# Loads on one queue in order of use, attention spread over the steps, and the LayerNorm statistics one step later

## Chip, cores, metric

One core of one Trainium2 chip. The metric is the device time of one execution in microseconds (us), lower is better. A single run over 1.5% above the fastest run of its kernel is called slow, and slow runs are left out of the ratios.

## The reference

Attention without softmax, an RMS norm of each head, then a two-layer MLP whose activation is h times softmax(h), with a LayerNorm in front of the second layer.

```python
kv  = einsum('bhsd,bhse->bhde', k, v)            # 8 batches, 8 heads, 576 tokens, 64 wide
out = einsum('bhsd,bhde->bhse', q, kv)
x   = out / sqrt(mean(out*out, -1) + 1e-6) * g_norm   # then [4608, 512]
h   = x @ w_in                                   # [4608, 1024]
solu = h * softmax(h)
ln  = (solu - mean(solu)) / sqrt(var(solu) + 1e-6) * g_ln
return ln @ w_out                                # [4608, 512]
```

## The kernel before

It works through nine blocks of 512 tokens: 512 of each of the eight batches, and a ninth block of what is left over. A block has eight pieces, each one `h_step` (four matmuls, exponential on ACT, product on DVE, square on POOL). I call eight pieces a stage. Stage c computes h of block c, the output of block c-1, and the attention of block c+1. LayerNorm is folded away: the second layer runs on u = h*exp(h) with centred weights, and each row is scaled at the end by a factor that needs three sums over its 1024 columns.

```python
def h_step(c, f):
    ...
    nc.scalar.activation(out=e[:, f % 2, :], in_=t[:, :], func=AF.Exp, ...)
    nc.vector.tensor_tensor(out=u_sb[c][:, f, :], in0=t[:, :], in1=e[:, f % 2, :], op=MUL)
    nc.gpsimd.tensor_tensor(out=usq_sb[c][:, f, :], in0=u_sb[c][:, f, :], in1=u_sb[c][:, f, :], op=MUL)
    if f % 2 == 1:
        nc.gpsimd.tensor_tensor(out=es_sb[c][:, f // 2, :], in0=e[:, 0, :], in1=e[:, 1, :], op=ADD)

def stats(c):
    ...   # 20 matmuls add usq, u and es into sum_ps
    nc.vector.tensor_copy(sums[:, :], t[:, :])
    st_ps = pst.tile([128, 4, 3], FP32, name="st_ps", tag="st")
    for m in range(4):
        nc.tensor.matmul(st_ps[:, m, :], sums[:, m * 128:(m + 1) * 128], stat_pick[:, :], ...)
    ...   # st, sq, var, vare on DVE; lv (Ln), rstd (Exp) on ACT

for c in range(NC + 1):
    for s in range(8):
        if c < NC: h_step(c, s)
        if c >= 1 and s == 0: stats(c - 1)       # sums, copy and transposition in one go
        if c == 0: ...   # s 0..3: scale w_out on POOL; s 5: its mean on PE; s 6, 7: centre it on DVE
        ...              # attention of block c+1: qT at 0 and 1, s_mm and o_mm at 2..5, kv at 6
        ...              # loads of block c+3 at s 2, 3, 4, issued by POOL
        if c >= 1:
            out_half(c - 1, s // 2, s % 2)
            if s % 2 == 1: out_evac(c - 1, s // 2)
```

The softmax here doesn't subtract the row's maximum and nothing guards it: scores larger than these inputs give would overflow.

## Time and profile before

| | before |
|---|---|
| time, median of 4 runs beside the changed kernel | 288.5 us (287.4 to 290.0) |
| span of the profiled run | 290.9 us (its time was 292.74, a slow run) |
| busy: PE, POOL, DVE, ACT | 220.5, 171.8, 140.0, 123.1 us |
| first h of stage 0 (its end), of stage 1 (its start) | 39.7, 66.8 us |

Here are the page's head, its first DMA queue, and one group of its costliest instructions: line, engine, operation, tiles, count, then busy time and mean in ns, then idle time before them.

```profile
span 290.9 us, 3927 instructions
...
PE 220.5 (76%) x1528; PEld 102.2 (35%) x1528; DVE 140.0 (48%) x251; ACT 123.1 (42%) x199; POOL 171.8 (59%) x171
...
q0 software_dynamic: 37632, 14.16, 42.1%
...
L269 ACT ACTIVATE lv<-vare,zero_t 128x4 f32<-128x4 f32 x9 | 2.7, 297 | 51.0 <-DVE vare L265 51.0
```

PE is busy for 76% of the span, but work that runs at half clock counts as busy too. The queue `q0`, which POOL issues, carries 14.2 MB; all weights come by another. The last line is the first half of the chain to the row factor: ACT waits 51.0 us for it in nine stages, so each of them stands at the end of a long chain.

The profiled run is a slow one, 4 us longer than the median. Stage lengths of before that are quoted below are of this slow run, and can be too long by 4 us in all.

### The profile page before, as it was taken

The numbers are of one execution on the slowest core, as the hardware profiler recorded it, in microseconds if no ns is written. First come the engines' busy times: TensorE is split into PE (matmuls) and PEld (weight loads), VectorE is DVE, ScalarE is ACT, GpSimd is POOL, SyncE is SP. The second block draws the span as 40 slices with busy tenths as digits, with TensorE's granted clock in tenths as the row PEclk, the third lists the DMA queues.
The fourth block names the chain that finished last, engine by engine and source line by source line (L and its number), as shares of the span: only waits on it lengthen the run. The fifth ranks groups of instructions, "written<-read, shape, count | busy, mean of one in ns | idle before, by whom it ended". The sixth has DMA issues, their size and how long they took to land.

```text
span 290.9 us, 3927 instructions
## 1 busy us (share of the span) xinstructions
PE 220.5 (76%) x1528; PEld 102.2 (35%) x1528; DVE 140.0 (48%) x251; ACT 123.1 (42%) x199; POOL 171.8 (59%) x171
## 2 busy tenths in 40 slices
PE   0014487455899799979897989899799798989792
PEld 0013033122444254434344434444344353344240
DVE  0503444309357325754672366357456646626422
ACT  1000738421087117713940394077169239513100
POOL 8624139997179907962994386257545727719700
PEclk9999999959599859997996699799999979979979
DMA  6999990296019901990796079101210201101114
GB/s 124 298 318 194 197 170 0 22 150 66 0 38 188 192 3 38 186 157 2 114 197 104 1 113 209 41 36 37 74 37 36 74 0 72 66 9 72 72 39 109
DMA packets 45763, 28.05 MB, mean 96 GB/s; under 512 B 15024, under 2 KB 39600, under 8 KB 45744
## 3 DMA queue, kind: packets, MB, share of 16 engines
q0 software_dynamic: 37632, 14.16, 42.1%
q1 hardware_dynamic: 8112, 13.64, 14.1%
q8 instruction: 12, 0.20, 0.3%
q14 instruction: 7, 0.06, 0.1%
HBM read 32.51 MB, written 9.44 MB: 144 GB/s over the span
## 4 chain that ended last, share of the span: by engine, by line
PE 37%; POOL 24%; ACT 13%; DMA 10%; DVE 7%; issue 6%; POOLq 0%; ACTq 0%; DVEq 0%
PE out_ps L280 14%; PE h_ps L227 10%; POOL usq_sb L236 9%; DMA vs<-in_v_dram 6%; POOL es_sb L238 6%; ACT e_sb L234 5%; PE st_ps L257 4%; DMA ks<-in_k_dram 4%; POOL w_out_g L320 4%; ACT rst L214 3%; PE qT_ps L184 3%; DVE u_sb L235 3%; ACT lss L212 3%; ACT osq L206 3%; DVE sums L254 2%
## 5 line engine op out<-in xcount | busy, mean ns | idle before, releaser
L236 POOL TENSOR_TENSOR usq_sb<-u_sb 128x512 bf16<-128x512 bf16 x72 | 75.0, 1043 | 87.4 <-DVE u_sb L235 87.3
L227 PE MATMUL h_ps<-x_sb,w_in_sb 128*128 128x512 bf16 x288 | 80.7, 405 | 0.8 <-DVE x_sb L215 0.8
L280 PE MATMUL out_ps<-w_out_sb,u_sb 128*128 128x512 bf16 x288 | 80.7, 411 | 0.0
L235 DVE TENSOR_TENSOR u_sb<-h_ps,e_sb 128x512 bf16<-128x512 f32 x72 | 49.6, 688 | 55.4 <-ACT e_sb L234 55.3
L234 ACT ACTIVATE e_sb<-h_ps,zero_t 128x512 f32<-128x512 f32 x72 | 49.3, 685 | 61.9 <-PE h_ps L227 61.9
L238 POOL TENSOR_TENSOR es_sb<-e_sb 128x512 bf16<-128x512 f32 x36 | 45.9, 1275 | 0.0
L227 PEld LDWEIGHTS <-w_in_sb 128*128 128x128 bf16 x288 | 29.8, 104 | 40.8 <-issue 12.0
L280 PEld LDWEIGHTS <-u_sb 128*128 128x128 bf16 x288 | 28.5, 104 | 37.2 <-issue 11.7
L215 DVE TENSOR_TENSOR x_sb<-o_ps,rst 128x512 bf16<-128x512 f32 x36 | 24.9, 691 | 34.2 <-ACT rst L214 34.2
L206 ACT ACTIVATE osq<-o_ps,zero_t 128x512 bf16<-128x512 f32 x36 | 24.2, 674 | 29.7 <-PE o_ps L199 29.7
L288 DVE TENSOR_SCALAR ob<-out_ps,rstd 128x512 f32<-128x512 f32 x36 | 26.7, 743 | 6.4 <-PE out_ps L280 6.4
L212 ACT ACTIVATE lss<-s_ps,eps_t 128x512 f32<-128x512 f32 x36 | 24.6, 683 | 10.4 <-PE s_ps L210 10.4
L214 ACT ACTIVATE rst<-lss,zero_t 128x512 f32<-128x512 f32 x36 | 26.0, 722 | 1.2
L269 ACT ACTIVATE lv<-vare,zero_t 128x4 f32<-128x4 f32 x9 | 2.7, 297 | 51.0 <-DVE vare L265 51.0
L210 PE MATMUL s_ps<-osq,head_mean 128*128 128x512 bf16 x36 | 14.7, 407 | 12.4 <-ACT osq L206 9.6
L152 PE MATMUL kv_ps<-vs,ks 128*64 128x64 bf16 x256 | 6.7, 214 | 15.7 <-DMA vs<-in_v_dram 15.7
L257 PE MATMUL st_ps<-stat_pick,sums 128*128 128x3 f32 x72 | 12.2, 292 | 7.2 <-DVE sums L254 7.2
L257 PEld LDWEIGHTS st_ps<-stat_pick,sums 128*128 128x128 f32 x72 | 11.4, 241 | 17.0 <-DVE sums L254 17.0
L249 PE MATMUL sum_ps<-usq_sb,stat_sel 128*32 128x512 bf16 x72 | 10.4, 384 | 8.8 <-POOL usq_sb L236 8.8
L184 PE MATMUL qT_ps<-ident,qs 128*64 128x128 bf16 x256 | 14.7, 285 | 2.6 <-DMA qs<-in_q_dram 2.6
L199 PE MATMUL o_ps<-qT_sb,kvbd 128*128 128x512 bf16 x32 | 13.5, 428 | 1.6 <-ACT lss L212 1.6
L189 DVE COPY qT_sb<-qT_ps 128x1024 bf16<-128x1024 bf16 x18 | 12.3, 685 | 4.4 <-PE qT_ps L184 4.1
(50 smaller groups left out, 149.7 us busy)
## 6 DMA issues: line engine op xcount, KB each, us to landing
out_dram<-ob SPq DMA_DIRECT2D x32, 256.0 KB, 2.3
ks<-in_k_dram POOLq DMA_DIRECT2D x8, 512.0 KB, 6.2
vs<-in_v_dram POOLq DMA_DIRECT2D x8, 512.0 KB, 9.7
qs<-in_q_dram POOLq DMA_DIRECT2D x8, 512.0 KB, 9.1
w_in_f<-in_moe_w_in_dram SPq DMA_DIRECT2D x4, 512.0 KB, 7.6
w_out_f<-in_moe_w_out_dram SPq DMA_DIRECT2D x4, 512.0 KB, 11.4
out_dram<-ob SPq DMA_DIRECT2D x8, 128.0 KB, 2.3
krem<-in_k_dram POOLq DMA_DIRECT2D x8, 64.0 KB, 12.4
```

Source lines behind the costliest of these rows:

```text
L206: nc.scalar.activation(out=osq[:, :], in_=t[:, :], func=AF.Square, bias=zero_t[:, :])
L212: nc.scalar.activation(out=lss[:, :], in_=t[:, :], func=AF.Ln, bias=eps_t[:, :])
L214: nc.scalar.activation(out=rst[:, :], in_=lss[:, :], func=AF.Exp, scale=-0.5, bias=zero_t[:, :])
L215: nc.vector.tensor_tensor(out=x_sb[c][:, p, :], in0=o_ps.pop(p)[:, :], in1=rst[:, :], op=MUL)
L227: nc.tensor.matmul(t[:, :], w_in_sb[:, dt, f * 128:(f + 1) * 128], x_sb[c][:, dt, :], start=(dt == 0), stop=(dt == NP - 1),)
L234: nc.scalar.activation(out=e[:, f % 2, :], in_=t[:, :], func=AF.Exp, bias=zero_t[:, :])
L235: nc.vector.tensor_tensor(out=u_sb[c][:, f, :], in0=t[:, :], in1=e[:, f % 2, :], op=MUL)
L236: nc.gpsimd.tensor_tensor(out=usq_sb[c][:, f, :], in0=u_sb[c][:, f, :], in1=u_sb[c][:, f, :], op=MUL)
L238: nc.gpsimd.tensor_tensor(out=es_sb[c][:, f // 2, :], in0=e[:, 0, :], in1=e[:, 1, :], op=ADD)
L257: nc.tensor.matmul(st_ps[:, m, :], sums[:, m * 128:(m + 1) * 128], stat_pick[:, :], start=True, stop=True)
L280: nc.tensor.matmul(t[:, :], u_sb[c][:, f, m * 128:(m + 1) * 128], w_out_sb[:, f, :], start=(f == 0), stop=(f == NF - 1),)
L288: nc.vector.tensor_scalar_mul(out=ob[:, :], in0=t[:, :], scalar1=rstd_sb[c][:, m:m + 1])
```

## The change

The intent: no load ahead of its use (one queue, in order of first use, w_in cast in flight and not scaled separately), no wait for the statistics (sums one piece later, their transposition two), and attention in even portions. The scheduling becomes a table of (stage, piece). Cut to its core:

```diff
-    for dt in range(NP):
-        nc.sync.dma_start(w_in_f[:, dt, :], moe_w_in[dt * 128:(dt + 1) * 128, :])
+    load_kv(0)
+    load_q(0)
+    for half in range(2):
+        nc.gpsimd.dma_start(w_in_sb[:, :, cols], moe_w_in[:, cols].rearrange("(n p) f -> p n f", p=128))
 ...
+    load_kv(1)
+    load_q(1)
+    for f4 in range(2):
+        nc.gpsimd.dma_start(w_out_f[:, 4 * f4:4 * f4 + 4, :], ...)
+    load_kv(2)
+    load_q(2)
 ...
-        t = pat.tile([128, NP, 128], FP32, name="kv_ps", tag="at")     # qT_ps likewise
+        t = pst.tile([128, NP, 128], FP32, name="kv_ps", tag="st")
 ...
-        nc.vector.tensor_tensor(out=x_sb[c][:, p, :], in0=o_ps.pop(p)[:, :], in1=rst[:, :], op=MUL)
+        nc.vector.scalar_tensor_tensor(
+            out=x_sb[c][:, p, :], in0=o_ps.pop((c, p))[:, :], scalar=g_rep[:, :], in1=rst[:, :], op0=MUL, op1=MUL
+        )
 ...
+    at(0, 3, kv_mm, 1) ...            # attention of block 1: kv 3, qT 4 and 5, s and o in 5 to 7
+    for f in range(NF):
+        at(0, 4 + f // 4, w_out_scale, f, nc.vector if f % 2 else nc.gpsimd)
+    at(0, 6, w_out_mean)
+    for f in range(NF):
+        at(0, 7, w_out_center, f)
+    for a in range(2, NC):
+        at(a - 2, 4 if a > 2 else 7, kv_mm, a)      # and kv_evac
+        at(a - 2, 5 if a > 2 else 7, qT, a, 0)
+        at(a - 2, 6 if a > 2 else 7, qT, a, 1)
+        at(a - 2, 7, o_mm, a, 0)
+        for p in range(NP):
+            at(a - 1, 2 * p, s_mm, a, p)
+            if p + 1 < NP:
+                at(a - 1, 2 * p + 1, o_mm, a, p + 1)
+    for c in range(NC):
+        at(c, 0, load_kv, c + 3); at(c, 1, load_q, c + 3); at(c, 2, load_rem, qrem, ...)
+        ...
+        at(c + 1, 1, stats, c)          # now only sums and their copy
+        at(c + 1, 2, stats_t, c)        # transposition and the row factor
+        at(c + 1, 3, out_evac, c, 0)    # then 4, 6, 7
```

## The prediction

> **What bounds the kernel now.** I read the page's rows of slices first (who is busy, at what clock), then the waits of all engines (who holds TensorE up), then the timeline of one block of 512 tokens and of the start, and last short stretches with their granted clock. I call a block's eight pieces of work (one `h_step` each) a stage; stage 0 fills the pipe, stages 1 to 8 are steady, stage 9 drains.
>
> ```profile
> PE   0014487455899799979897989899799798989792
> POOL 8624139997179907962994386257545727719700
> PEclk9999999959599859997996699799999979979979
> ```
>
> A slice is 7.3 us. PE is busy from the fifteenth slice on, but every third or fourth slice its granted clock is 5 to 7 tenths. The waits say what stands in front of those slices:
>
> ```profile
> PE kv_ps L152 <- DMA vs<-in_v_dram: 15.7, 1, 15.7
> PEld st_ps L257 <- DVE sums L254: 17.0, 9, 2.2
> PE s_ps L210 <- ACT osq L206: 9.6, 23, 1.3
> PE sum_ps L249 <- POOL usq_sb L236: 8.8, 12, 2.5
> PE mean_ps L326 <- POOL w_out_g L320: 7.1, 3, 5.2
> ```
>
> Once a stage, right after its first piece, PE wants the statistics of the block before. It waits for the last squares from POOL, then 0.8 us for the copy of the sums on DVE, with nothing else to do. The timeline around 100 us and the stretches show what this costs beyond the wait itself:
>
> ```profile
> 99.63 0.43 PE L249 MATMUL sum_ps<-usq_sb,stat_sel 128*32 128x512 bf16 x1 [0.61 <-POOL usq_sb L236]
> 102.23 1.87 PE L257 MATMUL st_ps<-stat_pick,sums 128*128 128x3 f32 x8 [0.78 <-DVE sums L254]
> ...
> 98.00:100.00 2.00, 0.74 (x9) 0.35 (x12) 0.50 (x1) 0.00 (x0) 2.00 (x3) 0.96 1.61 229
> 100.00:102.00 2.00, 1.45 (x13) 0.20 (x5) 0.51 (x1) 0.00 (x0) 1.81 (x2) 0.50 0.67 148
> 106.00:108.00 2.00, 2.00 (x7) 0.61 (x5) 0.00 (x0) 0.00 (x0) 0.00 (x0) 0.50 0.00 0
> ```
>
> PE was busy 0.74 of two us, then the clock is 0.50 until about 110, so roughly 10 us of work runs at half speed: four h matmuls take 1.71 us in the chain there, 0.86 to 0.88 elsewhere. The starts of the copy of `sums` give the stage lengths: 73.47, 101.49, 128.78, 156.04, 183.35, 208.66, 231.38, 255.35, 275.19, that is 28.0, 27.3, 27.3, 27.3, 25.3, 22.7, 24.0 and 19.8 us. The steady part is bound by PE, its waits, and the slow clock after them; the long stages are those whose loads keep POOL late. In pieces 2 to 5 ACT is nearly full (1.97 of 2.00 us from 86 to 92), and they last 2.5 to 2.9 us.
>
> The start is bound by loads. `vs` of block 0 reaches PE at 15.68 and its remainder at 22.90, as four loads of w_in and four of w_out share the engines. A second wait there matters for the change:
>
> ```profile
> 9.94 0.91 POOL L74 DMA_DIRECT2D ks<-in_k_dram  x1
> 12.90 0.87 POOL L74 DMA_DIRECT2D vs<-in_v_dram  x1 [2.06 <-DMA ks<-in_k_dram]
> 15.92 0.88 POOL L74 DMA_DIRECT2D qs<-in_q_dram  x1 [2.15 <-DMA vs<-in_v_dram]
> 31.54 0.88 POOL L74 DMA_DIRECT2D qs<-in_q_dram  x1 [1.91 <-DMA vs<-in_v_dram]
> ```
>
> The 9th load of POOL's queue starts when the 1st has landed, the 10th when the 2nd has, the 17th when the 9th has. POOL never has more than eight in flight, and it stands still meanwhile, its arithmetic too.
>
> **What the Trainium skill says.** "TensorE: Matmul & The Clock Gate", Part 1: PE's clock is gated to half unless the array was busy in the last window of about 3.4 us. The trace agrees: 0.50 follows the poor stretch, and 1.00 returns after some 10 us here. "DMA: Bandwidth & Descriptors", "Issuing engines are not separate DMA queues": queues interleave on the same 16 engines. The trace agrees: `ks` of block 0 took 11.4 us from issue, and the median of eight such loads is 6.2. "Perfetto Trace Analysis", "Identifying the Most-Contended Engine": matmul busy time overstates, as matmuls overlap. So I count starts: four h matmuls are 1.03 us busy, but the next group starts 0.86 after them.
>
> **The change, part by part.**
>
> Steady stages. Nothing is removed from PE; the order changes. By starts at full clock: h and out 16 groups of 0.863 = 13.8; eight s and o matmuls of 0.216 = 1.7; sums 20 at 0.055 and a gap of 0.1 = 1.2; `st_ps` 1.0; transposes 2 x 0.57 = 1.1; kv 0.9. Sum 19.8 us. Statistics now come after the second piece, some 3 us later than before, while POOL needs about 2.3 us (1.04 + 1.25) after the last u: that wait goes, and with it the slow clock. The copy of sums hides under piece 2 (1.9 us of PE work against 0.7). Attention has s in even and o in odd pieces, so ACT has 3.5 us per two pieces where PE has 3.9 or more. I followed one stage in order by these durations and found two new waits. First, the four small DVE operations on `st` stand behind x of piece 2, which waits for Ln and Exp; the two small ACT operations follow, and Exp of piece 3 and the square after it stand behind those, so s in piece 4 waits about 1.1 us. Second, `kv_evac` stands behind x of piece 4, and the transposes now use the same single PSUM buffer: about 0.7 us. So 19.8 + 1.8 = 21.6, say 21.7. POOL has 8.3 + 5.0 + at most 5.6 of issuing = 18.9 us, below that. Stage 6 has no kv (20.3), stage 7 no transposes (19.0), stage 8 no attention (16.5); stage 1 starts at half clock, +1.5. Sum: 23.2 + 4 x 21.7 + 20.3 + 19.0 + 16.5 = 165.8 us. Before, the first h of stage 1 starts at about 66.8 and the last h ends at 270.9: 204.1.
>
> g_norm on x: x becomes the form that `w_out_sb` shows at 0.74 instead of 0.69 us; 36 x 0.05 = 1.8 us of DVE, off the path. Four w_in scalings of 0.77 go.
>
> The end. Before, 20.0 us from the last h to the end. Now two halves of an output tile (1.7 us) run before the sums and one between sums and `st_ps`; the third tile then waits about 1.4 us for the first one's buffer. By the same following, 17.4.
>
> The start. One queue, one load (0.5 MB written from 1 MB read) per 2.7 us, as v1 follows k1 follows q0 before (25.9, 28.8, 31.5); the 64 KB pieces 0.5. From 1.24 plus 6 us: k0 7, v0 10, remainders 11, q0 13.5, w_in 19, k1 21.6, v1 24.3, q1 28, w_out 30.7 and 33.4, k2 36, v2 39, q2 42.6. Block 0's chain from first o to last x lasts 11 us (27.8 to 39.1 before), so first h ends near 28 and not 39.7. **But this is given back.** POOL does the square of piece 0 and then issues k3, v3 and two remainders, whose eighth predecessors are q1, w_out, w_out and k2: it is held to 36. After that it still has in its queue, ahead of w_out's last scaled piece, five squares, three pair sums, three more issues, and four scalings of 1.56: 5.2 + 3.8 + 2.4 + 6.2 = 17.6, so about 54. The mean of w_out (piece 6) is PE's next work and ends near 55. Piece 7 then holds in line: h at half clock 1.7; three rounds of s, Ln, Exp, square, o at 2.8 = 8.4 to x at about 65.5; eight centrings on DVE of 0.69 = 5.5, to 71; kv copy 0.9; two transposes at half clock, each followed by its copy through the one buffer, 3.4. First h of stage 1: 75.3, against 66.8. The start loses 8 us where it means to win 11.
>
> Sum: 75.3 + 165.8 + 17.4 = 258.5 us of span against 290.9. The timed median before is 288.83, or 0.993 of that span: 257 us.
>
> **Rivals.**
> - **The start hurts less or more.** If POOL is not held by the eight in flight, the mean comes near 45 and stage 1 starts near 62 to 65: 245. For it: loads may land faster without mixing. Against: the four lines above. If POOL's scalings are slowed by DVE's own four scalings beside them, 80 and 262.
> - **DVE and ACT in line become the bound.** Each wait I found comes from a strict order behind x, and x waits 2 us for ACT. Were it 3.5 us a stage in place of 1.8, eight stages cost 14 more: 270. For it: three consumers now share the one `st` buffer and need five turns a stage. Against: DVE has about 15 us and ACT 14 of work in 21.7.
> - **The clock does not come back.** If waits of 1 us are enough to halve it once a stage, each stage keeps 4 to 5 us: about 290, same as before. Against: from 195 to 222 the clock is 1.00 with waits of 0.3 to 0.8 us.
> - **All hides.** PE at its floor of 19.8 and a start as meant: about 235 to 240. Against: the single buffer and the order on DVE.
>
> **Range and chances.** The start is uncertain by 8 us either way, the steady part by 1 us a stage, about 7; together some 10. Time 257 us, range 247 to 269. Slower or within 2% needs two rivals at once, so faster by over 2% has 0.95, within 2% 0.04, slower 0.01.
>
> **What would show it.** Right: PE's clock near 1.00 from about 80 us on; copies of `sums` 21 to 22.5 us apart; no wait of `sum_ps` on POOL above 0.5 us; s waiting on osq once a stage; `mean_ps` waiting for w_out_g by over 10 us until about 55; POOL's issues of the remainders of block 3 waiting for w_out and k2; first h near 28 and stage 1 not before 70. Wrong: stage 1 starting before 65 or after 80, stages above 23 us, or 0.5 in the clock row after 85 us.

## The result, and the profile after

| | before | after |
|---|---|---|
| median of 4 runs, all fast | 288.5 us | 261.55 us (261.12 to 263.62) |
| ratio of fast runs | | 0.908 (95%: 0.901 to 0.914) |
| profiled span | 290.9 (slow) | 258.9 (fast) |
| first h of stage 0 (its end), of stage 1 (its start) | 39.7, 66.8 | 29.9, 76.84 |
| starts of `sums`, first and last | 73.47, 275.19 | 83.08, 246.28 |

Ratios are the mean time of one kernel's fast runs over the mean of the other's of the same rounds, so they are not quite the ratio of the medians. The four matmuls of the first h start in parts, as x comes: from 36.67 to 39.13 before, from 26.84 to 29.36 after. The predicted time was 257 us, the range 247 to 269.

The page of the kernel after, the same parts as before:

```profile
span 258.9 us, 3911 instructions
...
PE 197.2 (76%) x1528; PEld 93.5 (36%) x1528; DVE 145.9 (56%) x258; ACT 122.2 (47%) x199; POOL 166.8 (64%) x170
...
PE   0244793244259899979979979998997998997972
...
POOL 8543469983005976995997797565585584695800
PEclk9999999555559999999999999999999999999997
...
q0 software_dynamic: 39232, 17.30, 51.2%
...
L275 ACT ACTIVATE lv<-vare,zero_t 128x4 f32<-128x4 f32 x9 | 2.7, 297 | 20.9 <-DVE vare L271 20.9
```

PE is counted busy for 23 us less on the same 1528 matmuls, which fits the better clock (part of it may be the slow run before). From slice 13 on (a slice is 6.5 us) the clock row holds 9 up to the last slice. The five slices with 5 are the start, where PE now waits. `q0` carries the weights too. ACT's wait for the row factor fell from 51.0 to 20.9 us.

The waits of the kernel after (engine, tile and line, releaser: us in total, times, longest):

```profile
PE mean_ps L311 <- POOL w_out_g L304: 12.4, 4, 8.6
...
PE s_ps L210 <- ACT osq L206: 11.3, 10, 1.8
...
PE qT_ps L184 <- DVE kvbd L170: 8.9, 7, 7.1
...
PEld st_ps L263 <- DVE sums L256: 0.3, 1, 0.3
```

The wait of `st_ps` for the sums is 0.3 us in all, where it was 17.0 for the weight loads alone. `sum_ps` waits for POOL no more. What is left in the steady part is s behind its square and the transposes behind the copy of kv. The largest wait is now the mean of w_out in stage 0. In the timeline (start, duration, engine, line, then in brackets the idle time before it and who ended it), POOL first, PE after it:

```profile
34.64 0.69 POOL L82 DMA_DIRECT2D krem<-in_k_dram  x1 [0.34 <-DMA w_out_f<-in_moe_w_out_dram]
37.09 0.68 POOL L82 DMA_DIRECT2D vrem<-in_v_dram  x1 [1.76 <-DMA ks<-in_k_dram]
```

```profile
49.62 1.01 PE L311 MATMUL mean_ps<-w_out_g,col_mean 128*128 128x512 bf16 x2 [8.59 <-POOL w_out_g L304]
...
73.59 1.07 PE L184 MATMUL qT_ps<-ident,qs 128*64 128x128 bf16 x16 [7.09 <-DVE kvbd L170]
...
76.84 1.91 PE L229 MATMUL h_ps<-x_sb,w_in_sb 128*128 128x512 bf16 x4
...
111.28 0.38 PE L210 MATMUL s_ps<-osq,head_mean 128*128 128x512 bf16 x1 [1.39 <-ACT osq L206]
```

POOL's remainders of block 3 waited for w_out and ks as predicted, though only 0.34 and 1.76 us. The mean waited 12.4 us for the scaled weights (8.59, 0.54, 2.76, 0.53) and ended at 57.3. Centring ran from 67.33 to 72.67, the transposes of block 2 stood behind it for 7.09 us, and stage 1 began at 76.84. In the steady part, `s_ps` at 111.28 waits 1.39 us once a stage.

The starts of `sums` are 83.08, 104.30, 126.16, 148.02, 169.88, 191.09, 211.45, 230.07 and 246.28: stages of 21.2, 21.9, 21.9, 21.9, 21.2, 20.4, 18.6 and 16.2 us. Eight stages take 163.2 us, where before had 201.7 in its slow run. The start takes 9.6 us more (83.08 against 73.47), and the end, after the last copy of the sums, 3.1 less.

### The profile page after: what moved, and what is told of

The parts are those of the page before. It is cut to its first block, busy times and chain, and to the rows that moved or that the text cites. A ratio compares the mean times of both kernels' runs of the same rounds, so it can differ in the third digit from the quotient of the medians.

```text
span 258.9 us, 3911 instructions
## 1 busy us (share of the span) xinstructions
PE 197.2 (76%) x1528; PEld 93.5 (36%) x1528; DVE 145.9 (56%) x258; ACT 122.2 (47%) x199; POOL 166.8 (64%) x170
## 4 chain that ended last, share of the span: by engine, by line
PE 48%; ACT 18%; DVE 15%; POOL 9%; issue 4%; DMA 4%; POOLq 0%; ACTq 0%; DVEq 0%
PE h_ps L229 18%; PE out_ps L286 16%; ACT rst L214 5%; ACT lss L212 5%; PE qT_ps L184 4%; DVE x_sb L215 4%; ACT e_sb L236 4%; DMA qs<-in_q_dram 4%; PE sum_ps L251 4%; POOL usq_sb L238 3%; PE s_ps L210 2%; POOL w_out_g L304 2%; DVE kvbd L170 2%; DVE w_out_sb L314 2%; POOL es_sb L240 2%
## 5 line engine op out<-in xcount | busy, mean ns | idle before, releaser
L238 POOL TENSOR_TENSOR usq_sb<-u_sb 128x512 bf16<-128x512 bf16 x72 | 75.8, 1054 | 64.3 <-DVE u_sb L237 64.2
L229 PE MATMUL h_ps<-x_sb,w_in_sb 128*128 128x512 bf16 x288 | 78.7, 399 | 0.9 <-DVE x_sb L215 0.8
L286 PE MATMUL out_ps<-w_out_sb,u_sb 128*128 128x512 bf16 x288 | 73.2, 379 | 3.7 <-DVE ob L294 3.7
L215 DVE SCALAR_TENSOR_TENSOR x_sb<-o_ps,g_rep,rst 128x512 bf16<-128x512 f32 x36 | 27.0, 750 | 29.3 <-ACT rst L214 29.3
L229 PEld LDWEIGHTS <-w_in_sb 128*128 128x128 bf16 x288 | 28.5, 104 | 39.0 <-issue 12.0
L286 PEld LDWEIGHTS <-u_sb 128*128 128x128 bf16 x288 | 26.5, 98 | 37.3 <-issue 8.6
L212 ACT ACTIVATE lss<-s_ps,eps_t 128x512 f32<-128x512 f32 x36 | 24.6, 684 | 3.1 <-PE s_ps L210 3.1
L184 PE MATMUL qT_ps<-ident,qs 128*64 128x128 bf16 x256 | 11.9, 244 | 12.6 <-DVE kvbd L170 8.9
L184 PEld LDWEIGHTS <-qs 128*64 128x64 bf16 x256 | 9.4, 124 | 18.5 <-issue 16.2
L152 PEld LDWEIGHTS <-ks 128*64 128x64 bf16 x256 | 5.5, 123 | 23.2 <-issue 9.6
L311 PE MATMUL mean_ps<-w_out_g,col_mean 128*128 128x512 bf16 x8 | 4.0, 608 | 12.4 <-POOL w_out_g L304 12.4
L275 ACT ACTIVATE lv<-vare,zero_t 128x4 f32<-128x4 f32 x9 | 2.7, 297 | 20.9 <-DVE vare L271 20.9
```

The lines of the kernel that those rows point to most:

```text
L184: nc.tensor.transpose(t[hh * 64:hh * 64 + 64, pp, cols], qs[c][:, 2 * p + hh, j, :], ident[:, :])
L212: nc.scalar.activation(out=lss[:, :], in_=t[:, :], func=AF.Ln, bias=eps_t[:, :])
L215: nc.vector.scalar_tensor_tensor(out=x_sb[c][:, p, :], in0=o_ps.pop((c, p))[:, :], scalar=g_rep[:, :], in1=rst[:, :], op0=MUL, op1=MUL)
L229: nc.tensor.matmul(t[:, :], w_in_sb[:, dt, f * 128:(f + 1) * 128], x_sb[c][:, dt, :], start=(dt == 0), stop=(dt == NP - 1),)
L286: nc.tensor.matmul(t[:, :], u_sb[c][:, f, m * 128:(m + 1) * 128], w_out_sb[:, f, :], start=(f == 0), stop=(f == NF - 1),)
```

## The experiments

Eleven kernels ran, all correct. The "delayed-statistics kernel" is the first of them. My theory: the delayed statistics give the gain, by way of the clock; the start gives part of it back through POOL's queue, the mean and the centring; the steady part is left with a wait for s and one for kv. The rivals: the even attention or the order of loads gives the gain; the wait itself and not the clock is the cost; the start is bound by loads. Ratios are against before in the same rounds, three rounds unless said. In the first batch (delayed statistics alone, without the delay, loads later, centring later) the recorded ratios work out to a mean of 290.4 us for before, above each of its fast runs there (287.46 to 288.67), so slow runs are in that mean. Against those fast runs alone the four ratios are 0.905, 0.968, 0.883 and 0.897; the order of the kernels stays.

### The delayed statistics alone

```diff
-            if c >= 1 and s == 0:
-                stats(c - 1)
 ...
-                if s % 2 == 1:
-                    out_evac(c - 1, s // 2)
+                if s == 1: stats(c - 1)
+                if s == 2: stats_t(c - 1)
+                if s in (3, 4, 6, 7): out_evac(c - 1, {3: 0, 4: 1, 6: 2, 7: 3}[s])
```

(on the kernel before, with `stats` split in two as in the change)

> The kernel before with one part of the change alone: the sums are taken after the second piece of a stage, their transposition after the third piece, the output tiles scaled one step later. Theory (the wait for POOL at the sums, and the half clock that follows it, made the long stages): the clock row stays near full from stage 2 on, stages shrink from 25 to 28 us to about 22 to 23 (pieces 2 to 5 stay limited by ACT at 2.5 us), so 8 stages save about 25 us and the end about 2: 262 us. Rival (the loads that keep POOL busy are the cause, or ACT bounds the stages anyway): stages stay above 25 us in stages 1 to 5, total above 278 us.

Measured: 261.89 us, ratio 0.898 (0.886 to 0.911), span 256.9. Its clock row:

```profile
PEclk9999999996899999999999999999999999999997
```

(The profiled run is the fastest of its kernel, 3.1 us below the other two fast ones, at a clock of 0.981 against 0.965 and 0.966.) No half clock after the start. Stages are 22.1 five times, then 20.7, 19.6 and 16.2; `sums` starts at 77.13 first and 244.02 last. This one part has the whole gain. Against the changed kernel: the start is 5.95 us earlier (77.13 and 83.08), the eight stages take 166.9 us in place of 163.2, and the end is 0.3 us longer. So, in these two traces, the rest of the change wins 3.7 us in the steady part and loses 6 in the start; which part of the rest wins it is not separated here.

### The change without the delay

```diff
+        at(c + 1, 0, stats, c)
+        at(c + 1, 0, stats_t, c)
 ...
-        at(c + 1, 1, stats, c)
-        at(c + 1, 2, stats_t, c)
-        at(c + 1, 3, out_evac, c, 0)     # and 4, 6, 7
+            at(c + 1, 2 * m + 1, out_evac, c, m)
```

> The changed kernel with that part alone undone: sums and their transposition in the first piece again, output tiles scaled at the odd pieces. Theory: the wait on POOL and the 0.8 us for the copy of the sums come back in each stage, and with them the half clock; stages 25 to 27 us where loads run, 288 us or more in all, that is, nearly all of the gain is lost. Rival (spreading the attention is what gains): stages 22 to 23.5 us, total 265 to 272.

Measured: 279.42 us, ratio 0.961 (0.950 to 0.972). The direction is right and the size a miss: 18 of 27 us are lost, not all. Its profiled run was a slow one, so only the kinds of wait are read from it:

```profile
PEld st_ps L263 <- DVE sums L256: 20.0, 9, 2.6
...
PE sum_ps L251 <- POOL usq_sb L238: 1.5, 3, 0.9
```

The wait for the copy of the sums is back (17.0 before). The wait of the sums for POOL's squares is not: 1.5 us here, 8.8 before. I had expected both. The five full stages were 23.0 to 26.4 us in that slow run. So some 9 us remain won without the delay; I had put that down as none. Part of it is probably this wait: POOL issues the loads in pieces 0 to 2 now, not 2 to 4, and has caught up by the end of the stage. That was not tested alone, and neither was the even attention, which keeps ACT from filling pieces 2 to 5.

### Half clock or wait: filler work

```diff
+        for i in range(10):
+            nc.tensor.matmul(t[:, :], col_mean[:, :], w_in_sb[:, i % 4, 0:512], start=True, stop=True, ...)
         for n, (i, mov) in enumerate(todo):
```

(on the kernel before: ten matmuls whose results are overwritten, ahead of the sums)

> The kernel before with ten filler matmuls (128x128x512, results not used, some 2.2 us at full clock) on TensorE in each stage's wait for the last squares, ahead of the sums. Theory: the wait itself costs little over 1 us and the halved clock after it most of the loss; with TensorE kept busy the clock row stays at 9 or above through the stages, and a stage of 27.3 us becomes 23.5 to 24.5 in spite of more work: total 264 to 274. Rival: the loss is the wait itself and the serial order of the work: total unchanged, 286 to 290, or up to 10 us more.

Measured: 282.17 us, ratio 0.981 (0.976 to 0.986); more work, and 2% less time. The clock row, and three of the stretches that the prediction showed for before (busy us of each engine with instructions in brackets, then granted clock, DMA share, GB/s):

```profile
PEclk9999859956779999999999999999999999999999
```

```profile
98.00:100.00 2.00, 2.00 (x16) 0.71 (x14) 0.69 (x1) 0.38 (x1) 2.00 (x3) 1.00 1.34 256
100.00:102.00 2.00, 1.44 (x20) 0.33 (x12) 0.13 (x1) 0.00 (x0) 2.00 (x3) 1.00 1.49 213
...
106.00:108.00 2.00, 2.00 (x24) 1.18 (x24) 1.17 (x2) 1.38 (x2) 0.40 (x1) 1.00 0.00 0
```

The clock is 1.00 in each, where before had 0.96, 0.50 and 0.50. Two long stages compare: 101.87 to 126.45 is 24.6 us, against 27.3. The filler lies in the wait: from the start of the h ahead of it to the copy of the sums it is 5.3 us here (96.57 to 101.87) and 5.5 before (95.97 to 101.49), and PE still waits 0.78 us for the copy. So the kind of mechanism is shown: idle time of PE in this place costs the clock, and the clock costs time. How much is less sure. As read, the filler wins 2.7 us of the 5.2 that separate 27.3 from the 22.1 of delayed statistics; but before is a slow run here, and if all its 4 us of excess lay in the four long stages, it would be 1.7 of 4.2. Over the whole kernel and in fast runs the filler, which is work itself, won 5.7 us where the delay won 27.3. My expected total of 264 to 274 is a miss. Only three stages gained much (2.7, 1.8 and 2.7 us); the later ones are 23.6, 23.2 and 18.2 against 22.7, 24.0 and 19.8. The stage from the start (73.29 to 101.87, 28.6 us) did not gain, because the filler did not keep its clock up: it was 0.77, 0.50 and 0.88 in the stretches 72 to 76, 76 to 80 and 80 to 84 us (before: 0.56, 0.58, 1.00).

### Loads of block 3 later

```diff
-            at(c, 0, load_kv, c + 3)
-            at(c, 1, load_q, c + 3)
+            at(c, 0 if c else 6, load_kv, c + 3)
+            at(c, 1 if c else 6, load_q, c + 3)
 ...   # the remainders of q in stage 0 at piece 7
```

(on the kernel after)

> The changed kernel with the loads of block 3 and the first q remainder issued in pieces 6 and 7 of stage 0 and not in pieces 0 to 2. Theory (POOL stands in line behind loads that wait for the eighth load before them, and so scales w_out late): the last scaled piece comes at about 47 to 49 us and not at 56, and stage 1 starts 7 to 9 us earlier, near 68; total 253 us. Rival (w_out itself lands late, or POOL has too much arithmetic there): the mean still ends after 54 us, total unchanged within 1%.

Measured: 254.05 us, ratio 0.876 (0.866 to 0.886), span 251.1.

```profile
PE mean_ps L311 <- POOL w_out_g L304: 5.7, 4, 3.0
```

The mean of w_out waits 5.7 us in place of 12.4 and is done near 49; stage 1 starts at 68.45 in place of 76.84. The time falls by 7.5 us. POOL's queue holds up stage 0, as predicted. In the kernel after, POOL waited 2.1 us for earlier loads to land (0.34 and 1.76), and issuing k, v, q and four remainders took it some 5.75 us, which is the larger share.

### Centring later

```diff
-    for f in range(NF):
-        at(0, 7, w_out_center, f)         # ahead of the kv copy and transposes of block 2
 ...
+    for f in range(NF):
+        at(0, 7, w_out_center, f)         # behind them
```

> The changed kernel with the eight centrings of w_out placed after the copies for block 2 on DVE, not before them. Theory (they stand in line before the copies that PE waits for, 7.1 us): that wait falls below 1.5 us and the first h of stage 1 starts near 71; but the first output tile now waits for the centrings and u for all of them, so only 2.5 to 4 us stay: 258 us. Rival (all eight are needed anyway before PE can go on): no gain, 261.5 us.

Measured: 258.4 us, ratio 0.890 (0.879 to 0.900). Stage 1 starts at 71.89, and the longest wait of the transposes falls from 7.1 to 1.8 us. Of the 5 us won at that point 3 stay, as the first u of stage 1 stands behind the centring now, until 77.47. The stage after the first copy of the sums is 22.4 us in place of 21.2; in it `var`, a DVE operation on 4 elements a partition, takes 1.18 us in place of 0.16 (the section on attention in its old places tells what stands beside it).

### Loads in the old order

```diff
-    for half in range(2):
-        nc.gpsimd.dma_start(w_in_sb[:, :, cols], ...)
+    for dt in range(NP):
+        nc.sync.dma_start(w_in_f[:, dt, :], moe_w_in[dt * 128:(dt + 1) * 128, :])
+    ...   # four loads of w_out the same way; the remainders of two batches together, as before
+    for dt in range(NP):
+        nc.vector.tensor_copy(w_in_sb[:, dt, :], w_in_f[:, dt, :])
```

> The changed kernel with the loads of the start back in their old order and on two queues, w_in copied to bf16 on DVE; statistics and attention as changed. First h back at about 39.5 from 26.8. Theory (stage 1 waits for POOL to scale w_out, and the first h's 12 us are lost in that wait): the mean of w_out ends at 58 to 61 and not at 57, total 262 to 266. Rival (the loads in order carry through): the start is 11 us later, total 272.

Measured: 270.42 us, ratio 0.939 (0.932 to 0.945); against the changed kernel's 261.55, 9 us slower. I had expected 262 to 266, since by my prediction the early first h is given back; that was wrong. The new order of loads carries most of its gain into the end time. (Not all 9 us need lie in the start: in the slow trace the first `sums` came 7.1 us later than after, and stages 2 to 4 were 23.4 to 24.2 us; the edit also loads remainders in pairs, as before.) So two things of opposite sign meet in the start: the loads in order win some 7 us or more, and the new plan of stage 0 (mean at piece 6, all centring behind all attention, block 2 behind that) loses more. Only the sum was as predicted. Its profiled run is a slow one; the first h of stage 1 came at 83.4 in it, 6.6 us later than after.

### Attention in its old places

```diff
-            at(a - 2, 4 if a > 2 else 7, kv_mm, a)     # kv_evac too
-        at(a - 2, 5 if a > 2 else 7, qT, a, 0)
-        at(a - 2, 6 if a > 2 else 7, qT, a, 1)
-        at(a - 2, 7, o_mm, a, 0)
+            at(a - 2, 6 if a > 2 else 7, kv_mm, a)
+        at(a - 1, 0, qT, a, 0)
+        at(a - 1, 1, qT, a, 1)
+        at(a - 1, 1, o_mm, a, 0)
         for p in range(NP):
-            at(a - 1, 2 * p, s_mm, a, p)
-                at(a - 1, 2 * p + 1, o_mm, a, p + 1)
+            at(a - 1, 2 + p, s_mm, a, p)
+                at(a - 1, 2 + p, o_mm, a, p + 1)
```

(and kv and the transposes in their old PSUM buffers)

> The changed kernel with the attention of blocks 2 to 8 back in its old pieces and its old PSUM buffers; loads and statistics as changed. Theory (spreading takes the limit of ACT in pieces 2 to 5 away, worth 0.3 to 0.9 us a stage, and costs at the start, as block 2 must be transposed before stage 1): stages of 22.1 us, as in the kernel before with delayed statistics, 5 to 6 us lost over the stages; first h of stage 1 about 4 us earlier, at 73; total 262 us. Rival (spreading is what keeps the stages short): stages above 23.5, total above 270.

Measured: 268.0 us, ratio 0.927 (0.918 to 0.936); 6.5 us slower than after, where I had expected nothing. Stage 1 begins at 65.14, 11.7 us earlier than after and 8 earlier than I had expected, as the transposes of block 2 stand in stage 1 again and not ahead of it; at the first `sums` (77.10) 6.0 us of that are left. But the stages are 22.8, 24.5, 24.2, 24.0, 22.2, 20.8, 21.4 and 16.2, where I had expected 22.1. The timeline and two stretches of one of them:

```profile
103.76 0.17 DVE L267 TENSOR_TENSOR sq<-st 128x8 f32<-128x8 f32 x1
...
103.81 1.06 POOL L238 TENSOR_TENSOR usq_sb<-u_sb 128x512 bf16<-128x512 bf16 x1
103.96 0.93 DVE L269 TENSOR_TENSOR var<-st,sq 128x4 f32<-128x4 f32 x1
...
108.28 0.38 PE L210 MATMUL s_ps<-osq,head_mean 128*128 128x512 bf16 x1 [2.41 <-ACT osq L206]
```

```profile
106.00:108.00 2.00, 0.00 (x0) 0.00 (x0) 1.00 (x2) 1.97 (x4) 1.07 (x2) 1.00 1.60 193
...
110.00:112.00 2.00, 2.00 (x6) 0.72 (x5) 1.41 (x2) 0.72 (x2) 0.82 (x1) 0.50 0.36 126
```

`var` is a DVE operation on 4 elements a partition. The same kind took 0.17 us just before (`sq`), and took 0.93 here: it started 0.15 us after POOL's square and ended at 104.89, with that square (104.87). Behind `var` stand `vare`, the two small ACT operations, and then ACT's whole line; the next s waits 2.41 us. PE is idle from 106 to 108, and the clock is halved by 110 to 112. In the delayed-statistics kernel the same wait is 1.59 us, and the clock row there holds 9. "SBUF — State Buffer" of the Trainium skill, "Who interferes with whom", states that a DVE instruction with two SBUF inputs and a GpSimd instruction that reads SBUF shut each other out, the later one waiting to the end of the first; the 0.02 us between the two ends agrees. That this makes the stages here longer than in the delayed-statistics kernel fits, but was not tested alone.

It is tempting to read a limit between 1.6 and 2.4 us of idle time out of this. The traces do not bear it out. A later wait of this same run, and one of the delayed-statistics kernel, each with a stretch after it:

```profile
223.23 0.38 PE L210 MATMUL s_ps<-osq,head_mean 128*128 128x512 bf16 x1 [1.61 <-ACT osq L206]
...
225.00:227.00 2.00, 2.00 (x6) 0.76 (x5) 1.41 (x2) 0.67 (x3) 0.76 (x1) 0.50 0.34 122
```

```profile
74.62 0.38 PE L199 MATMUL o_ps<-qT_sb,kvbd 128*128 128x512 bf16 x1 [2.24 <-DVE qT_sb L189]
...
76.00:78.00 2.00, 2.00 (x25) 0.83 (x18) 0.69 (x1) 0.00 (x0) 1.51 (x2) 1.00 0.00 0
```

The wait of 1.61 us was followed by half clock, three of 1.64 us in the same run were not, and the one of 2.24 us was not. The length of one wait does not decide it; what does is not shown.

### One SBUF input in the small chain (five rounds)

That gave a theory for something the prediction lacked: in the kernel after, the three stages in which POOL issues loads take 21.9 us and the one without loads 21.2.

```diff
-        nc.vector.tensor_tensor(out=sq[:, :, :], in0=st[:, :, 1:3], in1=st[:, :, 1:3], op=MUL)
-        nc.vector.tensor_tensor(out=var[:, :], in0=st[:, :, 0], in1=sq[:, :, 0], op=SUB)
+        nc.vector.tensor_tensor(out=sq[:, :, :], in0=st_ps[:, :, 1:3], in1=st[:, :, 1:3], op=MUL)
+        nc.vector.tensor_tensor(out=st_ps[:, :, 3], in0=st_ps[:, :, 0], in1=sq[:, :, 0], op=SUB)
 ...   # vare reads st_ps[:, :, 3] in place of var
```

> The changed kernel, with the small VectorE operations of the LayerNorm chain reading one of their two inputs from PSUM, so that none of them reads SBUF twice. Theory: the loaded stages (those in which POOL computes the norms of the next block's q and k) are 21.9 us long against 21.2 in the unloaded one because such an operation stands still while POOL computes. Then three stages lose some 0.65 us each: 261.5 becomes 259 to 260, and the stages are 21.2 to 21.3 each. Rival: the loaded stages are longer for another reason (ScalarE or VectorE being busier with the next block's work): 261 to 262, stages still 21.9.

(The words in brackets there are loose: each block's k and q come already cast, and POOL issues loads; it computes no norm of them.)

Measured: 259.19 us, ratio 0.899 (0.897 to 0.901), six fast runs from 258.44 to 259.57, all below the lowest of the kernel after. POOL's sum and DVE's `sq` in a loaded stage, in the kernel after and then in this one:

```profile
107.69 1.29 POOL L240 TENSOR_TENSOR es_sb<-e_sb 128x512 bf16<-128x512 f32 x1
...
108.20 0.81 DVE L267 TENSOR_TENSOR sq<-st 128x8 f32<-128x8 f32 x1
```

```profile
108.35 1.30 POOL L240 TENSOR_TENSOR es_sb<-e_sb 128x512 bf16<-128x512 f32 x1
...
108.87 0.17 DVE L267 TENSOR_TENSOR sq<-st_ps,st 128x8 f32<-128x8 f32 x1
```

In both, `sq` starts beside the sum. With two SBUF inputs it takes 0.81 us and ends at 109.01, as the sum does (108.98); with one it takes 0.17. All stages with full attention are now 21.21 us. The theory is shown: 3 times 0.65 us is 1.95 of the 2.4 us between the medians.

### kv ahead of s

```diff
-            at(a - 2, 4 if a > 2 else 7, kv_mm, a)
-            at(a - 2, 4 if a > 2 else 7, kv_evac, a)
+            plan[a - 2, 4] = [(kv_mm, (a,)), (kv_evac, (a,))] + plan.get((a - 2, 4), [])   # a > 2
```

> The changed kernel with kv and its copy put ahead of s in piece 4 of each stage; all else as it was. Theory (the two waits left in a stage come from the order in line: s waits 0.75 to 1.4 us for the square, and the transposes 0.3 us for the kv copy that stands behind x): kv fills the first wait and its copy runs ahead of x, so stages fall from 21.2 or 21.8 to 20.1 to 20.5 us, five of them with kv: 256 to 257 us. Rival (the stage is limited by DVE and ACT work as a whole, and a wait filled here opens elsewhere): stages stay above 21 us, 261 us.

Measured: 257.48 us, ratio 0.896 (0.891 to 0.901). The gain is as expected, less about 1 us: the three loaded stages stayed at 21.1, where 20.1 to 20.5 was expected. The kv matmuls fill the time in which s waits: stages of 20.5, 21.1, 21.1, 21.1, 20.5, then 20.4, 18.6, 16.2. The wait of s in piece 4 of a loaded stage falls from 1.39 to 0.52 us, and the transposes no longer wait for the copy of kv. Both steady waits of the prediction are shown to be real time, about 0.75 us a stage together.

### Two versions that beat both

The first: loads of block 3 later, kv ahead of s, centring placed between the rounds of s, and w_out scaled on ACT alone. The reason for the last is in the kernel after, in stage 0:

```profile
41.87 5.24 DVE L304 TENSOR_SCALAR w_out_g<-w_out_f,g_ln_sb 128x512 bf16<-128x512 f32 x2
...
47.04 0.67 DVE L237 TENSOR_TENSOR u_sb<-h_ps,e_sb 128x512 bf16<-128x512 f32 x1
```

Two scalings on DVE, of 512 elements a partition each, took 5.24 us beside POOL's work; those of w_in in the kernel before, of 1024 elements, took 0.77 each. POOL's own took 1.56 each, as before. Meanwhile u of piece 6 waited until 47.04.

```diff
-        eng.tensor_scalar_mul(out=w_out_g[:, f, :], in0=w_out_f[:, f, :], scalar1=g_ln_sb[:, f:f + 1])
+        nc.scalar.activation(out=w_out_g[:, f, :], in_=w_out_f[:, f, :], func=AF.Copy, scale=g_ln_sb[:, f:f + 1])
```

> A version meant to be better: loads of block 3 in pieces 6 and 7, kv first in piece 4, w_out scaled on ACT and not on POOL and DVE, centrings between the rounds of s and after the copies. Theory (the start is a line behind POOL and DVE, the loads themselves are done for the mean at 35): mean ends near 42, stage 1 starts near 56 to 60, stages 20.3: 236 to 241 us. Rival (w_out or block 2 land too late for it): mean not before 48, total above 245.

Measured: 239.62 us, ratio 0.833 (0.829 to 0.837). The mean ends at 43.2, and stage 1 starts at 57.60.

The second adds the one-input chain, and moves kv and the transposes of block 2 into the rounds of s, half of the centring behind the first piece of stage 1.

```diff
+    at(0, 7, kv_mm, 2)              # between the rounds of s, p = 1 and 2
+    at(0, 7, kv_evac, 2)
 ...
+    at(0, 7, qT, 2, 0)              # and centrings 0, 1; then after the last s: qT(2, 1) and 2, 3
 ...
+    for f in range(4, NF):
+        at(1, 0, w_out_center, f)
```

> The best try so far (239.6 us) with the small LayerNorm operations reading one input from PSUM, and with part of the centring and the transpositions of stage 0 moved into the rounds of s and x there. If both theories hold (stage 0 is a chain through mean and centring, loaded stages wait for a blocked VectorE operation): first h of stage 1 at 52 to 54 us in place of 57.6, loaded stages 20.5 in place of 21.1, total 231 to 235. If only the first: 235. If neither: 239 to 240.

Measured: 233.29 us (231.69 to 234.27), ratio 0.810 (0.806 to 0.813). Two rows of its page:

```profile
PE   0046588769999999999999999999979989998971
...
PEclk9999999976999999999999999999999999999999
```

First h of stage 1 at 52.48, stages of 20.5 five times, 20.1, 18.6 and 15.6: both theories held. PE is full from slice 10 on.

## Why the prediction was right

| step | predicted | measured |
|---|---|---|
| end of the first h of stage 0 | near 28 | 29.9 |
| POOL held by loads in flight | to 36 | 0.34 + 1.76 us, to 37.1 |
| mean of w_out done | near 55 | 57.3 |
| last x of stage 0; centrings done | 65.5; 71 | 67.3; 72.67 |
| first h of stage 1 | 75.3 | 76.84 |
| steady stages | 21.7 each | 21.2, three of 21.9, 21.2 |
| s in piece 4 behind its square | about 1.1 | 0.75, in loaded stages 1.39 |
| transposes behind the copy of kv | about 0.7 | 0.27 |
| first to last h | 165.8 | about 165.2 (76.84 to 242.0) |
| end | 17.4 | 16.9 |
| span | 258.5 | 258.9 |
| time | 257 | 261.55 |

**"That wait goes, and with it the slow clock."** Right, and it is all of the net gain: the delay alone gives 261.89 us. The filler shows that the clock is a real part (2.7 of 5.2 us in a long stage as read, 1.7 of 4.2 if the slow state of before is put against it); the rest, the wait and the serial order after it, is not divided further. "Roughly 10 us of work runs at half speed" suggests 5 us lost by the clock alone; that is more than the filler gave back. And the rival "The clock does not come back" was nearer than its chance says: in fast runs, waits of 1.61 us (attention in its old places) and of 1.11 us (filler, at 74.02) were followed by half clock. That waits of 1.39 us in the kernel after were not is measured, not understood; in this the prediction was lucky.

**"DVE and ACT in line" behind x.** Right in kind: both waits exist, and putting kv first takes them away. Their sum was 1.8 us in the prediction; it measured 1.0 us without loads and 1.7 with them. What I did not see is why the loaded stages are longer: a DVE operation with two SBUF inputs stands beside POOL's work. Without these 3 times 0.65 us the stages would have come out 2.6 us below the sum, not 0.6, so their closeness is partly luck.

**"But this is given back."** Right in the sum: stage 1 starts 10 us later than before. Loads issued later on POOL win 8.4 us there and centring later 5, so the path through POOL, the mean and DVE is shown. With the attention in its old places the first `sums` come 6 us earlier. Wrong in one reading of it: the early loads are not lost. Without them the kernel is 9 us slower.

**The hold by eight loads in flight** ended about when I said (37.1 for 36), for another reason in part: waiting made 2.1 us of it, POOL's own issuing the rest. And the rival that had POOL's scalings slowed by DVE's was the wrong way round: DVE's were slowed, to 5.24 us for two.

**The last factor is the step that was off.** "0.993 of that span" sets a median of fast runs against the span of a slow profiled run (its time was 292.74, 1.8 us above its span). The changed kernel's profiled run took 261.15 us for a span of 258.9, 2.25 more. With that the same sum gives 260.8. All other errors together are 0.4 us, as the start was 1.5 us longer and the stages and the end 1.1 shorter.

Left open: how the 9 us that remain won without the delay divide; how the gain of the delay divides between the clock and the wait; and what pattern of idle time halves the clock.

## What to carry to other kernels

Where PE waits once an iteration for a result that another engine is about to finish, move the consumer one step later before anything else: here this alone saved 9.5% in fast runs. Part of that is the clock: filling the wait with useless matmuls, and changing nothing else, saved 2%. After such a change look at the fill of the pipe and at the small chains: what stands in an engine's line ahead of the next stage's first operand cost up to 24 us here (stage 1 at 76.84 and at 52.48), and a tiny DVE operation with two SBUF inputs took 0.8 to 1.2 us in place of 0.17 beside POOL. And compare a span with the time of the same run before you turn one into the other.

## What the Trainium skill lacked or had wrong

- "TensorE: Matmul & The Clock Gate", Part 1, gives an idle window of about 3.4 us before the clock is halved. Here waits of 2.41, 1.61 and 1.11 us were followed by half clock, while others of 2.24 and 1.64 us were not. In the kernel before, around 98 us, idle pieces of 1.11 and 0.61 us with thin work between them were enough, and the clock stayed at 0.50 until about 110, some 8 us after the last wait there ended at 102.23. The page's remark that the window runs free of the work may cover it; no run here tests that. The page also tells of short idle times between groups of matmuls that bring the clock down, but gives no lengths for them.
- "SBUF — State Buffer", "Who interferes with whom": agrees, and has no figure for tiny operations. A DVE operation on 4 or 8 elements a partition took 0.93 and 0.81 us beside POOL, in place of 0.17, and ended 0.02 and 0.03 us after POOL's (centring later: 1.18 us, also 0.02 after).
- No page that I read has the limit of eight loads in flight on POOL's queue. From the ninth load on POOL often stood until the load eight before it had landed: 1.52 to 2.44 us before; in the kernel after, 1.28 to 2.33 us in the loads of the start, and 0.34 and 1.76 us for block 3. Whether the limit is the hardware's or the program's, these traces do not show.
